# Second-layer weights loaded at other places, a third buffer for finished attention rows and for an expert's first 128 tokens, and other PSUM banks for the early-row transposes

## Chip, cores and metric

The kernel runs on one core of one Trainium2 chip. The metric is the device time of one execution in microseconds (us); lower is better.

## The reference

Block-sparse attention feeds a mixture of experts. Shapes: 4 batches, 8 heads, 768 positions, head size 64, blocks of 32 positions; 3072 tokens of 512 features; 8 experts with a hidden size of 1024.

```python
scores = q @ k.T / 8            # kept where |block_i - block_j| <= 1, where either block is
attn = softmax(scores) @ v      # the first or the last, and at 3 sampled key blocks per query block
x = attn as (3072, 512)
do = x @ w_skip > 0             # the other tokens leave as they are
e = argmax(x[do] @ w_gate); gate = softmax(x[do] @ w_gate)[e]
out[do] = x[do] + gate * (relu(x[do] @ w1[e]) @ w2[e])
```

## The kernel before

The program has two stages, and the order of the work in both is written out by hand.

**Attention.** 16 dense units (first and last query block) are followed by 44 sparse units: 22 query blocks, two units (`b` = 0 and 2) each. `sparse_step(k)` runs a software pipeline over the units: scores of unit k+2 on TensorE (`S`), row maxima on VectorE (`M`), exponentials on ScalarE (`X`), transposes (`T`, `V`) of unit k+1, the product with the values (`A`, L468) of unit k, and the normalisation (`N`, L479 to L481) and the stores (`after`, L489) of unit k-1. `N` writes a tile `xs` of finished rows, one per query block, from a pool with two buffers; `after` writes that tile to `out` with four DMAs from SyncE (SP) and transposes it on VectorE (L498) for the router. Between these, `work(q)` gives out single steps of the routing (`route`: logits, arg-max, rank, list entries) and of `look_first` (L573), which fetches the first 256 tokens of the biggest expert before attention ends and transposes them (`rows`, L596, into `xeh`, `xel`). Routing and the early transposes use one PSUM bank, `ps_r`, in turn. `fill(q)` issues loads and splits at hand-chosen steps; the last twelve weight quarters (w1 of expert 0, w2 of expert 0, w1 of expert 1) are issued there in that order, four for each matrix.

All fp32 matrices of the experts are multiplied as a high and a low part: `split_w` copies 512 columns to the high part on ScalarE (L526) and subtracts on VectorE or GpSimd (POOL) (L528). The raw weights stand in the tile that held the keys (`kts`), as a ring of three places of 2 MB: place (2p - 1) mod 3 for w1 of expert p, 2p mod 3 for w2. So a load waits until the matrix that stood there has been split or used.

**Experts.** They run one after the other, the biggest first. A `tc.Switch` jumps to code for the expert's number of tokens; each engine jumps by itself (register load of the count, branch on L1301). The first `Switch` (L1197, `arm == 0`) runs expert 0 on the early rows, with the last routing steps (`beside`) between its matmuls; `splits` cuts w2 of expert 0 from its fourth hidden slice on. Expert p then does `gemm1` (L840 to L842, one PSUM bank of five per slice `f`; `each(f)` splits slice f of its w2 beside it), the part product of its last chunk, `turn()` (transposes of the next expert's gathered rows, L630), and `gemm2` for the other chunks. `close` scales, adds the row and scatters it (L923, L73). `gather` fetches 128 rows of `out` by an indirect DMA from POOL's queue (L618); every expert has three such row tiles, in two sets that alternate. Around the end of expert p, POOL's program order is: gathers of expert p+2's second and third 128 rows, split of the next w1's last slice, load of w2 of expert p+2 (L522), end of the arm, `close_first(p)`: scatter of the first 128 rows, gather of expert p+2's first 128 rows; then the arm of expert p+1. SP loads w1 of expert p+2 in the middle of expert p.

Of the kernel before, what the change touches and what calls it, by code (L numbers as in the profile page):

```python
# [13 lines left out]
ALU = mybir.AluOpType  # L14
# [31 lines left out]
def tile_kernel(ctx, tc, qs, qd, kt, v, sb, wg, w1, w2, out):  # L46
# [368 lines left out]
    class Sparse:  # L415
# [57 lines left out]
        def N(self):  # L473
            if self.b == 0:
                Sparse.xs[self.i] = rt.tile([P, B, 2, D], F32, name="xs", bufs=2)
            xs = Sparse.xs[self.i]
            rs = ap.tile([P, 2, 2, 1], F32, name="rs")
            return [
                lambda: nc.vector.tensor_single_scalar(out=rs, in_=self.op[:, :, :, D:VD], scalar=1e-9, op=ALU.add),  # L479
                lambda: nc.vector.reciprocal(out=rs, in_=rs),  # L480
                lambda: nc.vector.tensor_tensor(out=xs[:, self.b:self.b + 2], in0=self.op[:, :, :, 0:D], in1=rs.broadcast_to([P, 2, 2, D]), op=ALU.mult),  # L481
            ]
# [90 lines left out]
    def look_first():  # L573
# [22 lines left out]
        def rows(c):  # L596
            if c == 0:
                early["t"] = [rt.tile([P, NK1, 2 * P], F32R, name=n) for n in ("xeh", "xel")]
            xh, xl = early["t"]
            tp = ps_r.tile([P, NK1, P], F32, name="rps")  # L600
            for k in range(NK1):
                nc.tensor.transpose(out=tp[:, k, :], in_=early["x"][c][:, P * k:P * k + P], identity=ident)
            cs = slice(P * c, P * c + P)
            late.append(lambda: nc.scalar.copy(out=xh[:, :, cs], in_=tp))
            after_late.append(lambda: V.tensor_tensor(out=xl[:, :, cs], in0=tp, in1=xh[:, :, cs].bitcast(F32), op=ALU.subtract))
# [92 lines left out]
    def fill(q):  # L698
# [55 lines left out]
    def sparse_step(k):  # L754
# [193 lines left out]
    def order_lists(lt=lt, lsw=lsw, size=CS):  # L948
# [24 lines left out]
    def halves(p, c, y):  # L973

        wh, wl = wview("2", p)
        cs, a = slice(P * c, P * c + P), p * CS + c
        o = os[y]
        for z in range(2):
            zs = slice(256 * z, 256 * z + 256)
            yp = yps[(y + z) % 2][:, 0:256]  # L980
            for f in range(NK2):
                for n, (l, r) in enumerate(((hh, wh), (hh, wl), (hl, wh))):
                    nc.tensor.matmul(out=yp, lhsT=l[:, f, cs], rhs=r[:, f, zs], start=(f + n == 0), stop=(f == NK2 - 1 and n == 2))
            nc.vector.scalar_tensor_tensor(out=o[:, zs], in0=yp, scalar=ltf[:, a, 1:2], in1=xs[p % 2][c][:, zs], op0=ALU.mult, op1=ALU.add)
            scatter_to(out=out.rearrange("n (z c) -> (n z) c", z=2), out_offset=bass.IndirectOffsetOnAxis(ap=ends[:, c, z:z + 1], axis=0),
                       in_=o[:, zs], in_offset=None, bounds_check=2 * N - 1, oob_is_err=False)
# [5 lines left out]
    def last_chunk(p, n, first, turn):  # L992

        def chunk(c):
            xg = xs[p % 2][c]
            with tc.If(n > CG * c + 2) as most:
# [25 lines left out]
    def full_chunks(p, n):  # L1022

        def chunk(c, last=False):
            if p == E - 1 and last:
                halves(p, c, c)
                return
            gemm2(p, c, c)
            close(p, c, c, xs[p % 2][c])
            fetch_rows(p + 2, c)  # L1030
# [15 lines left out]
    def outputs(p, n):  # L1046
# [6 lines left out]
        def turn():  # L1053
            if p + 1 < E:
                columns(xs[(p + 1) % 2], x)

# [4 lines left out]
        full_chunks(p, n)  # L1061
        if p + 2 < E:
            load_w("2", p + 2, eng=nc.gpsimd)

# [3 lines left out]
    def expert(p, n, nxt):  # L1068

        if n > CG:  # L1070
            gemm1(p, x, G * n, parts(p), few=G * (n % CG) if n % CG < 3 else 0)
# [11 lines left out]
        def turn():  # L1083
            if p + 1 < E:
                columns(xs[(p + 1) % 2], x)

# [4 lines left out]
        if p == E - 1:  # L1091
            product(p, c, G * (n - CG * c), 1)
            for y in range(c):
                if y == c - 1:
                    halves(p, y, y)
                else:
                    gemm2(p, y, y)
                    close(p, y, y, xs[p % 2][y])
            return
# [11 lines left out]
        if c == 2:  # L1111
            gemm2(p, 1, 1)
            close(p, 1, 1, xs[p % 2][1])
            fetch_rows(p + 2, 1)
        if n > 2:
            gemm2(p, 0, 0)
        if p + 2 < E:
            load_w("2", p + 2, eng=nc.gpsimd)
        announce(p + 1, nxt)

    def product(p, c, m, z):
        if m > 64:
            gemm2(p, c, z)
            close(p, c, z, xs[p % 2][c])
        else:
            gemm2_few(p, c, m, z)
            close(p, c, z, xs[p % 2][c], m)

    def gather_parts(p, m, z):

        xg, gate = xs[p % 2][0], ltf[0:m, p * CS, 1:2]
# [16 lines left out]
    def beyond():  # L1148
# [18 lines left out]
        for e in range(E):  # L1167
            a = e * LC
            n = tokens_of(e)
            with tc.If(n > CG * CS):  # L1170
# [4 lines left out]
                with tc.For_i(CS, (n + (CG - 1)) // CG, 2) as c:  # L1175
                    cur = mp.tile([P, 2, 2], I32, name="cur", bufs=1)
                    nc.vector.tensor_copy(out=cur, in_=ltx[:, bass.ds(c + a, 2), :])
                    gx = xs[0][:2]
                    for z in range(2):
# [9 lines left out]
    wt.update({"2" + t: wp2.tile([P, 4096], F32R, name=f"w2{t}") for t in "hl"})  # L1189
    xs = [[mp.tile([P, DM], F32, name=f"x{z}{c}", bufs=1) for c in range(CS)] for z in range(2)]  # L1190
    for z in range(2):
        for c in range(CS):
            nc.gpsimd.memset(xs[z][c], 0.0)
    os = [mp.tile([P, DM], F32, name=f"o{z}", bufs=1) for z in range(2)]
    yps = [ps_y.tile([P, DM], F32, name=f"yp{z}", bufs=1) for z in range(2)]
    x = [mp.tile([P, NK1, CS * P], F32R, name=n, bufs=1) for n in ("xh", "xl")]
    for arm in tc.Switch(nc.values_load(small, min_val=0, max_val=1), 2, hint="first"):  # L1197
        if arm == 0:
            px, p0, p1, d1, d1b, d2, d2b, rank, d3, d4, d5, d5b, put, d6 = last[0]()
            le, leg = early["l"]  # L1200
            load_w("2", 1, 0, 2)

# [18 lines left out]
            gemm2(0, 1, 1, range(0, 6))  # L1221
            keep_x(turn_x(xs[0][2:], ps_h, "hp"), *early["t"])
# [5 lines left out]
            columns(xs[1], x)  # L1228
            for z in range(NEAR):
                split_w("1", 1, z, 8)  # L1230
            load_w("1", 2)
            with tc.If(n0 > 2 * CG):
                gemm2(0, 0, 0)
                close(0, 2, 0, xs[0][2])
            rows(2, range(CS))
            load_w("2", 2, eng=nc.gpsimd)
        else:
            load_w("2", 1)
            for step in last[0]():
# [6 lines left out]
            clear()  # L1246
            columns(xs[0], x)
            n0 = tokens_of(0)
# [64 lines left out]
```

## Time and profile before

| | us |
|---|---|
| median of 3 runs | 526.8 (521.44 to 530.41) |
| profiled execution, whole | 517.92 |
| its span | 516.3 |
| attention, to the last row product | about 248 of it |
| TensorE busy | 448.1 (87%) |
| VectorE, ScalarE, GpSimd busy | 316.6, 247.1, 150.4 |

Times in rows are us from the span's start. PE is TensorE's matmul part, PEld its weight load, PEq or PEldq its sequencer, SP the engine that only issues DMAs. In a row the bracket tells how long the engine was idle before and what it waited for; "issue" means that it waited for nothing that the profile shows. A granted clock of 1.00 is 2.4 GHz, 0.50 is 1.2 GHz. DMA share is the mean busy share of the 16 DMA engines.

### The profile page before, as it was taken

How to read it: one execution, taken by the hardware profiler on the slowest of the kernel's cores; microseconds unless marked ns; L12 is line 12 of the kernel's file. 1: busy time of each engine (PE TensorE's matmuls, PEld its weight loads, DVE VectorE, ACT ScalarE, POOL GpSimd, SP SyncE). 2: the span in 40 equal slices, each digit the busy share in tenths (PEclk: the TensorE clock that was granted, in tenths of full speed). 3: DMA queues.
4: the chain of work that ended last, by engine and by line, in shares of the span. 5: the costliest groups of instructions: out<-in, count | busy, mean ns of one | idle time of the engine just before them, and what ended most of it. 6: DMA issues, size and time to landing. Idle time of an engine off the chain costs nothing. (4 is left out here: it accounts for less than half of the span.)

```text
span 516.3 us, 17305 instructions
## 1 busy us (share of the span) xinstructions
PE 448.1 (87%) x6594; PEld 350.5 (68%) x6594; DVE 316.6 (61%) x819; ACT 247.1 (48%) x576; POOL 150.4 (29%) x215
## 2 busy tenths in 40 slices
PE   5999998879897989997277899999999966799992
PEld 2777776656675766665167679796888853777982
DVE  2887756766776686965428257658387833494610
ACT  2444466665665666766214065455372705451500
POOL 2003333442424343433710503412314123122011
PEclk9999999999999999999678999999999987999997
DMA  8999969886989787879960605754634662811001
GB/s 283 345 274 251 222 146 225 199 217 178 222 222 228 183 221 195 216 192 284 323 224 2 241 25 182 258 207 172 233 143 150 229 228 76 329 43 48 0 18 40
DMA packets 48599, 96.48 MB, mean 187 GB/s; under 512 B 8167, under 2 KB 34920, under 8 KB 43554
## 3 DMA queue, kind: packets, MB, share of 16 engines
q1 hardware_dynamic: 43744, 73.39, 50.1%
q0 software_dynamic: 4240, 20.67, 11.6%
q8 instruction: 67, 1.10, 0.9%
q14 instruction: 114, 0.93, 0.6%
q10 hardware_dynamic: 434, 0.39, 0.2%
HBM read 85.03 MB, written 12.19 MB: 188 GB/s over the span
## 5 line engine op out<-in xcount | busy, mean ns | idle before, releaser
L455 ACT COPY pt<-tp 128x512 f32<-128x512 f32 x88 | 52.5, 599 | 57.3 <-PE tp L449 56.4
L442 ACT ACTIVATE pr<-sp,m 128x256 f32<-128x256 f32 x176 | 69.3, 483 | 2.0 <-DVE m L436 2.0
L436 DVE TENSOR_REDUCE m<-sp 128x2 f32<-128x512 f32 x88 | 56.6, 685 | 19.3 <-PE sp L429 18.3
L845 ACT ACTIVATE hh<-hp 128x256 fp32r<-128x256 f32 (+2 forms) x56 | 21.4, 381 | 89.4 <-PE hp L842 83.7
L840 PE MATMUL hp<-xh,w1h 128*128 128x256 f32 (+3 forms) x192 | 58.0, 302 | 6.1 <-DVE hl L848 2.8
L841 PE MATMUL hp<-xl,w1h 128*128 128x256 f32 (+3 forms) x192 | 57.5, 299 | 0.3 <-DVE x L1133 0.3
L429 PE MATMUL sp<-kg,q 64*32 64x256 f32 x1408 | 52.6, 386 | 5.5 <-issue 5.0
L842 PE MATMUL hp<-xh,w1l 128*128 128x256 f32 (+3 forms) x192 | 57.4, 299 | 0.0
L73 POOL DMA_INDIRECT out<-o,lt x17 | 16.8, 989 | 132.5 <-DVE o L923 89.3
L449 PEld LDWEIGHTS tp<-ident,pr 128*128 128x128 f32 x352 | 37.8, 141 | 23.0 <-issue 10.7
L449 PE MATMUL tp<-ident,pr 128*128 128x128 f32 x352 | 49.3, 281 | 4.4 <-issue 3.4
L468 PE MATMUL op<-vb,pt 128*32 128x65 f32 x1376 | 46.2, 222 | 6.1 <-issue 5.7
L468 PE MATMUL op<-va,pt 128*32 128x65 f32 x1376 | 47.0, 225 | 3.0 <-issue 2.0
L848 DVE SCALAR_TENSOR_TENSOR hl<-hp,hh 128x256 fp32r<-128x256 f32 (+2 forms) x56 | 23.4, 418 | 39.9 <-ACT hh L845 22.8
L906 PE MATMUL yp<-w2h,hh 128*128 128x512 f32 x112 | 45.0, 402 | 0.0
L908 PE MATMUL yp<-w2h,hl 128*128 128x512 f32 x112 | 44.3, 396 | 0.0
L907 PE MATMUL yp<-w2l,hh 128*128 128x512 f32 x112 | 44.3, 395 | 0.0
L212 POOL COPY kg<-kts 128x512 f32 x66 | 40.8, 628 | 6.5 <-POOL kg L212 2.3
L840 PEld LDWEIGHTS hp<-xh,w1h 128*128 128x128 f32 x192 | 36.0, 188 | 9.3 <-issue 6.2
L468 PEld LDWEIGHTS op<-va,pt 128*32 128x32 f32 x1376 | 33.4, 111 | 10.4 <-issue 9.0
L528 DVE TENSOR_TENSOR w2l<-kts,w2h 128x512 fp32r<-128x512 f32 x56 | 38.3, 688 | 3.2 <-ACT w2h L526 1.5
L468 PEld LDWEIGHTS op<-vb,pt 128*32 128x32 f32 x1376 | 34.9, 111 | 7.7 <-issue 7.7
(214 smaller groups left out, 909.4 us busy)
## 6 DMA issues: line engine op xcount, KB each, us to landing
va<-v SPq DMA_DIRECT2D x48, 260.0 KB, 4.9
vb<-v SPq DMA_DIRECT2D x48, 260.0 KB, 4.5
kts<-w SPq DMA_DIRECT2D x6, 2048.0 KB, 8.3
kts<-w POOLq DMA_DIRECT2D x6, 2048.0 KB
vt<-v SPq DMA_DIRECT2D x16, 390.0 KB, 7.5
kts<-w SPq DMA_DIRECT2D x12, 512.0 KB, 6.2
kts<-kt SPq DMA_DIRECT2D x15, 384.0 KB, 7.9
q<-qs SPq DMA_DIRECT2D x22, 256.0 KB, 3.6
```

The costliest lines, as they stand in the source:

```text
L429: nc.tensor.matmul(out=self.sp[w][32 * a:32 * a + 32, g], lhsT=qt[self.i][ws, p, :], rhs=kg[self.x][ws, p, :], start=True, stop=True)
L436: return [lambda w=w: nc.vector.tensor_reduce(out=self.mx[:, w], in_=self.sp[w], axis=AX.X, op=ALU.max, negate=True) for w in range(2)]
L442: nc.scalar.activation(out=self.pr[:, g, w], in_=self.sp[w][:, g], func=AF.Exp, bias=self.mx[:, w, g:g + 1])
L449: nc.tensor.transpose(out=tp[:, u, :], in_=self.pr[:, g, u // 2, (u % 2) * P:(u % 2) * P + P], identity=ident)
L455: nc.scalar.copy(out=self.pt[:, g], in_=self.tp[g])
L468: nc.tensor.matmul(out=self.op[32 * a:32 * a + 32, g, w, :], lhsT=self.pt[:, g, 2 * w + t, 32 * a:32 * a + 32], rhs=vt[:, 8 * (self.b + g) ...
L840: nc.tensor.matmul(out=hp[:, 0:w], lhsT=wh[:, f, k, :], rhs=xh[:, k, 0:w], start=(k == 0), stop=False)
L841: nc.tensor.matmul(out=hp[:, 0:w], lhsT=wh[:, f, k, :], rhs=xl[:, k, 0:w], start=False, stop=False)
L842: nc.tensor.matmul(out=hp[:, 0:w], lhsT=wl[:, f, k, :], rhs=xh[:, k, 0:w], start=False, stop=(k == NK1 - 1))
L906: nc.tensor.matmul(out=yp, lhsT=hh[:, f, cs], rhs=wh[:, f, :], start=(f == 0), stop=False)
L907: nc.tensor.matmul(out=yp, lhsT=hh[:, f, cs], rhs=wl[:, f, :], start=False, stop=False)
L908: nc.tensor.matmul(out=yp, lhsT=hl[:, f, cs], rhs=wh[:, f, :], start=False, stop=(f == NK2 - 1))
```

## The change

- `Sparse.N`: the tile of finished rows gets three buffers instead of two.
- `look_first`: the early transposes go to the two banks of `ps_t` (tile `tp`) instead of the one of `ps_r`.
- `sparse_step`: in the step after the last unit the routing step is run before `N` instead of after it.
- `fill` issues only w1 of expert 0. The four quarters of w2 of expert 0 are issued after the attention loop, w1 of expert 1 as one load at the start of the first arm.
- Experts: the first 128 rows have three buffers (`x0`), the other two chunks two (`x12`). `fetch_rows(p + 2, 0)` moves from `close_first(p)` to the start of expert p, and the load of w2 of expert p+2 from the end of expert p to the start of expert p+1, behind that gather.

```diff
-                Sparse.xs[self.i] = rt.tile([P, B, 2, D], F32, name="xs", bufs=2)
+                Sparse.xs[self.i] = rt.tile([P, B, 2, D], F32, name="xs", bufs=3)
...
-            tp = ps_r.tile([P, NK1, P], F32, name="rps")
+            tp = ps_t.tile([P, NK1, P], F32, name="tp")
...
-        for y in ([2 * z, 2 * z + 1] if 0 <= z < 2 else [z + 2] if 2 <= z < 10 else []):
-            which, p = (("1", 0), ("2", 0), ("1", 1))[y // 4]
-            load_w(which, p, y % 4, 4)
+        for y in ([2 * z, 2 * z + 1] if 0 <= z < 2 else []):
+            load_w("1", 0, y, 4)
...
-        mix(units[k - 1].N(), [])
+        if k < nu:
+            mix(units[k - 1].N(), [])
         pe, soon, then, pool = work(q)
         mix(soon, [])
+        if k == nu:
+            mix(units[k - 1].N(), [])
...
         run((pe, soon + then, lambda: [l() for l in pool]))
+    for y in range(4):
+        load_w("2", 0, y, 4)
     att.close()
...
+    def xr(p):
+        return [x0[p % 3]] + x12[p % 2]
+
     def rows(p, cr):
         for c in cr:
-            gather(xs[p % 2][c], lt[:, p * CS + c, 0:1])
+            gather(xr(p)[c], lt[:, p * CS + c, 0:1])
...
     def expert(p, n, nxt):
 
+        fetch_rows(p + 2, 0)
+        if p + 1 < E:
+            load_w("2", p + 1, eng=nc.gpsimd)
         if n > CG:
...
         if n > 2:
             gemm2(p, 0, 0)
-        if p + 2 < E:
-            load_w("2", p + 2, eng=nc.gpsimd)
         announce(p + 1, nxt)
...
-        close(p, 0, 0, xs[p % 2][0])
-        fetch_rows(p + 2, 0)
+        close(p, 0, 0, xr(p)[0])
...
-    xs = [[mp.tile([P, DM], F32, name=f"x{z}{c}", bufs=1) for c in range(CS)] for z in range(2)]
-    for z in range(2):
-        for c in range(CS):
-            nc.gpsimd.memset(xs[z][c], 0.0)
+    x0 = [mp.tile([P, DM], F32, name=f"x{z}0", bufs=1) for z in range(3)]
+    x12 = [[mp.tile([P, DM], F32, name=f"x{z}{c}", bufs=1) for c in range(1, CS)] for z in range(2)]
+    for t in x0 + x12[0] + x12[1]:
+        nc.gpsimd.memset(t, 0.0)
...
             le, leg = early["l"]
+            load_w("1", 1)
             load_w("2", 1, 0, 2)
...
             rows(2, range(CS))
-            load_w("2", 2, eng=nc.gpsimd)
         else:
+            load_w("1", 1)
             load_w("2", 1)
```

Elsewhere `xs[p % 2][c]` is replaced by `xr(p)[c]`.

## Rows read from the trace of the kernel before

**Rows 1.** Busy time by stage: window, its length, busy us and instruction counts of each engine, granted TensorE clock, DMA share, GB/s.
```profile
242.00:248.00 6.00, 2.59 (x126) 2.16 (x119) 0.34 (x2) 2.66 (x5) 4.59 (x4) 1.00 1.05 396
248.00:254.00 6.00, 1.49 (x11) 0.96 (x11) 4.04 (x13) 2.66 (x5) 2.25 (x3) 0.52 0.99 327
261.00:267.00 6.00, 5.81 (x31) 4.76 (x32) 0.42 (x1) 0.94 (x2) 0.00 (x0) 0.64 0.97 337
428.00:436.00 8.00, 4.52 (x18) 2.99 (x20) 3.07 (x5) 2.81 (x7) 3.07 (x3) 0.57 0.41 119
```

**Rows 2.** Timeline of VectorE at the end of attention: start, duration, line and operation, and the idle time before it.
```profile
248.27 0.42 DVE L481 TENSOR_TENSOR xs<-op,rs 128x256 f32<-128x256 f32 x1 [4.86 <-DMA out<-xs]
251.55 0.69 DVE L605 TENSOR_TENSOR xel<-rps,xeh 128x512 fp32r<-128x512 f32 x1 [1.34 <-ACT xeh L604]
252.90 0.89 DVE L307 TENSOR_TENSOR lsb<-pos,rows_of 128x384 f32<-128x384 int32 x1
```

**Rows 3.** Timeline of SP's DMA issues over the same stretch (x4 merges four issues).
```profile
235.78 3.74 SPq L522 DMA_DIRECT2D kts<-w  x4
239.62 2.57 SPq L489 DMA_DIRECT2D out<-xs  x4
242.98 4.03 SPq L522 DMA_DIRECT2D kts<-w  x4
247.67 1.87 SPq L489 DMA_DIRECT2D out<-xs  x4
250.71 3.81 SPq L522 DMA_DIRECT2D kts<-w  x4
254.61 3.39 SPq L489 DMA_DIRECT2D out<-xs  x4
```

**Rows 4.** Timeline of TensorE from the last row products to the first expert.
```profile
248.00 0.31 PE L468 MATMUL sp<-vb,pt 128*32 128x65 f32 x6 [3.41 <-issue]
249.78 1.11 PE L602 MATMUL rps<-ident,xe 128*128 128x128 f32 x4 [1.46 <-DVE xel L605]
253.94 1.48 PE L325 MATMUL rps<-phi,lsb 128*128 128x48 f32 x6 [3.04 <-DVE lsb L307]
261.19 0.57 PE L840 MATMUL hp<-xeh,w1h 128*128 128x256 f32 x1 [5.77 <-issue]
```

**Rows 5.** The branches of TensorE's sequencer, line L1301, each in a window of its own around one Switch: count, duration in ns (least, median, most), first and last start. The first is the jump into the first arm, the others those of experts 1, 5 and 6.
```profile
L1301 PEldq COMPARE_BRANCH  x1: 6195/6195/6195, 254.8 to 254.8; - x1
L1301 PEldq COMPARE_BRANCH  x2: 301/1344/2386, 306.3 to 307.8; - x2
L1301 PEldq COMPARE_BRANCH  x2: 437/3415/6393, 410.5 to 411.6; - x2
L1301 PEldq COMPARE_BRANCH  x2: 317/1434/2552, 434.8 to 435.9; - x2
```

**Rows 6.** ScalarE and POOL around the first arm: copies and subtractions for the weight splits, and the clearing of the row tiles.
```profile
270.81 0.61 ACT L526 CAST w2h<-kts 128x512 fp32r<-128x512 f32 x1
252.11 5.25 POOL L528 TENSOR_TENSOR w1l<-kts,w1h 128x512 fp32r<-128x512 f32 x4 [3.75 <-ACT w1h L526]
257.30 2.86 POOL L1193 MEMSET x<- 128x512 f32 x6
286.38 1.03 POOL L618 DMA_INDIRECT x<-out,lt  x1 [26.23 <-DVE lt L952]
```

**Rows 7.** The weight loads of line L522 as a whole: time from issue to landing.
```profile
DMA to landing us min/median/max: 5.0/6.3/8.3
```

**Rows 8.** TensorE around experts 5 and 6.
```profile
406.90 1.09 PE L630 MATMUL hp<-ident,x 128*128 128x128 f32 x8
418.41 0.47 PE L862 MATMUL hp<-w1h,xh 128*128 128x512 f32 x1 [4.38 <-issue]
431.48 1.97 PE L630 MATMUL hp<-ident,x 128*128 128x128 f32 x8 [4.40 <-DMA x<-out,lt]
434.23 4.48 PE L918 MATMUL yp<-kts,hf 128*64 128x512 f32 x16
451.24 0.41 PE L840 MATMUL hp<-xh,w1h 128*128 128x320 f32 x1 [2.75 <-DVE hl L848]
456.72 3.65 PE L918 MATMUL yp<-kts,hf 128*64 128x512 f32 x16
```

**Rows 9.** POOL's timeline from the end of expert 4 on.
```profile
413.77 1.17 POOL L618 DMA_INDIRECT x<-out,lt  x1 [0.30 <-DVE w1l L528]
418.07 0.60 POOL L522 DMA_DIRECT2D kts<-w  x1 [1.83 <-issue]
426.79 1.01 POOL L73 DMA_INDIRECT out<-o,lt  x1 [8.12 <-issue]
428.11 1.06 POOL L618 DMA_INDIRECT x<-out,lt  x1 [0.30 <-issue]
444.20 0.59 POOL L522 DMA_DIRECT2D kts<-w  x1 [3.60 <-DVE w1l L528]
```

**Rows 10.** VectorE at the start of expert 6, and SP's loads of w1 of experts 6 and 7.
```profile
450.76 0.42 DVE L848 SCALAR_TENSOR_TENSOR hl<-hp,hh 128x256 fp32r<-128x256 f32 x1 [4.52 <-issue]
407.17 0.35 SPq L522 DMA_DIRECT2D kts<-w  x1
438.92 0.35 SPq L522 DMA_DIRECT2D kts<-w  x1
```

More of the change, by code (lines that the diff above doesn't have):

```diff
@@ L983, in halves @@
                     nc.tensor.matmul(out=yp, lhsT=l[:, f, cs], rhs=r[:, f, zs], start=(f + n == 0), stop=(f == NK2 - 1 and n == 2))
-            nc.vector.scalar_tensor_tensor(out=o[:, zs], in0=yp, scalar=ltf[:, a, 1:2], in1=xs[p % 2][c][:, zs], op0=ALU.mult, op1=ALU.add)
+            nc.vector.scalar_tensor_tensor(out=o[:, zs], in0=yp, scalar=ltf[:, a, 1:2], in1=xr(p)[c][:, zs], op0=ALU.mult, op1=ALU.add)
             scatter_to(out=out.rearrange("n (z c) -> (n z) c", z=2), out_offset=bass.IndirectOffsetOnAxis(ap=ends[:, c, z:z + 1], axis=0),
@@ L994, in chunk @@
         def chunk(c):
-            xg = xs[p % 2][c]
+            xg = xr(p)[c]
             with tc.If(n > CG * c + 2) as most:
@@ L1028, in chunk @@
             gemm2(p, c, c)
-            close(p, c, c, xs[p % 2][c])
+            close(p, c, c, xr(p)[c])
             fetch_rows(p + 2, c)
@@ L1054, in turn @@
             if p + 1 < E:
-                columns(xs[(p + 1) % 2], x)
+                columns(xr(p + 1), x)
         last_chunk(p, n, lambda: split_next((0, 1)), turn)
@@ L1084, in turn @@
             if p + 1 < E:
-                columns(xs[(p + 1) % 2], x)
+                columns(xr(p + 1), x)
         c = (n - 1) // CG
@@ L1097, in expert @@
                     gemm2(p, y, y)
-                    close(p, y, y, xs[p % 2][y])
+                    close(p, y, y, xr(p)[y])
             return
@@ L1112, in expert @@
             gemm2(p, 1, 1)
-            close(p, 1, 1, xs[p % 2][1])
+            close(p, 1, 1, xr(p)[1])
             fetch_rows(p + 2, 1)
@@ L1116, in expert @@
             gemm2(p, 0, 0)
-        if p + 2 < E:
-            load_w("2", p + 2, eng=nc.gpsimd)
         announce(p + 1, nxt)
@@ L1123, in product @@
             gemm2(p, c, z)
-            close(p, c, z, xs[p % 2][c])
+            close(p, c, z, xr(p)[c])
         else:
             gemm2_few(p, c, m, z)
-            close(p, c, z, xs[p % 2][c], m)
+            close(p, c, z, xr(p)[c], m)
     def gather_parts(p, m, z):
-        xg, gate = xs[p % 2][0], ltf[0:m, p * CS, 1:2]
+        xg, gate = xr(p)[0], ltf[0:m, p * CS, 1:2]
         for j in range(1, P // m):
@@ L1177, in beyond @@
                     nc.vector.tensor_copy(out=cur, in_=ltx[:, bass.ds(c + a, 2), :])
-                    gx = xs[0][:2]
+                    gx = xr(0)[:2]
                     for z in range(2):
@@ L1221, in tile_kernel @@
             gemm2(0, 1, 1, range(0, 6))
-            keep_x(turn_x(xs[0][2:], ps_h, "hp"), *early["t"])
+            keep_x(turn_x(xr(0)[2:], ps_h, "hp"), *early["t"])
             gemm2(0, 1, 1, range(6, NK2))
@@ L1227, in tile_kernel @@
                 gemm1_tokens(0, early["t"])
-            columns(xs[1], x)
+            columns(xr(1), x)
             for z in range(NEAR):
@@ L1233, in tile_kernel @@
                 gemm2(0, 0, 0)
-                close(0, 2, 0, xs[0][2])
+                close(0, 2, 0, xr(0)[2])
             rows(2, range(CS))
-            load_w("2", 2, eng=nc.gpsimd)
         else:
+            load_w("1", 1)
             load_w("2", 1)
@@ L1246, in tile_kernel @@
             clear()
-            columns(xs[0], x)
+            columns(xr(0), x)
             n0 = tokens_of(0)
```

## The prediction

> **What bounds the kernel now.** I read the page's slices first, then busy time by stage, then the timelines of single engines where TensorE is idle, then the branches of its sequencer. TensorE is the bound nearly everywhere (87% of the span), so the change can pay only where TensorE stands still. There are two such places that it touches.
>
> The first is the end of attention. From 242 to 248 TensorE works 2.59 of 6 us, from 248 to 254 only 1.49, with the DMA engines saturated (share 1.05 and 0.99), and the clock falls to half [rows 1]. VectorE shows why: the normalisation of the last block's first unit waits 4.86 us, from 243.41 to 248.27, for the stores of the tile whose buffer it takes over [rows 2]. With two buffers that is the block before the previous one, whose four stores SP issued only at 239.62, behind four weight quarters [rows 3]. Behind the waiting instruction on VectorE stands the subtraction that frees the single `ps_r` bank, so the second early transposition waits 1.46 us more, to 249.78 [rows 4]. From there a chain runs through ScalarE, the subtraction (to 252.24), the last normalisation, the routing's one-hot rows (L307, to 253.79), the `put` matmuls at 253.94 and the jump into the first arm, which takes TensorE's sequencer 6.2 us, to the first expert matmul at 261.19 [rows 2, 4, 5].
>
> The second is experts 5 and 6. Before expert 6's rows are transposed TensorE waits 4.40 us for a gather [rows 8], which POOL issued at 428.11, behind a scatter that came 8.12 us after the load of w2 of expert 6 [rows 9]. In 428 to 436 the clock is 0.57 of full [rows 1]. Inside expert 6 a further 2.75 us go, while VectorE is between two arms and idle 4.52 us [rows 8, 10].
>
> **The change, part by part. End of attention.** A third buffer makes the last block wait for the block three back, stored long before: 4.86 us of waiting go, and VectorE's next work starts at 243.4. The early transposes in `ps_t` no longer need the subtraction. What is late next is TensorE's own stream: it stands 3.41 us in the middle of a run of equal matmuls, without a semaphore, from 244.59 to 248.00 [rows 4]. I take this, like the 6.2 us jump, for a wait for instructions while the DMA engines are full, since jumps take 2.4 and 2.55 us in quiet stretches but 6.4 where a 2 MB weight load had been issued at 407.17, 4.4 us earlier [rows 5, 10]. Without w2 of expert 0, issued at 242.98 before [rows 3], the DMA engines have only the rest of w1 and small stores in 244 to 252. So I take 1.0 us for the stall (bounds 0 and 3.41) and 2.6 us for the jump (bounds 2.4 and 6.2).
>
> The new chain: the stall would start at 244.6; it and the last six matmuls end the row products at 245.8; the second transposition follows. From its start to the `put` it took 4.16 us (249.78 to 253.94); the three normalisation operations now follow L307 instead of preceding it, which saves 0.75, and at full clock the transposition is some 0.3 shorter: 3.1 us, so `put` at 248.9. The jump begins 0.86 us later as before (253.94 to 254.8): 249.8, plus 2.6, plus the 0.2 before the first matmul (254.8 + 6.2 to 261.19): 252.6. The gain is 261.19 - 252.6 = **8.6 us**. Bounds: both waits as before give 244.6 + 3.4 + 0.2 + 3.1 + 0.86 + 6.2 + 0.2 = 258.6, a gain of 2.6; none and 2.4 give 251.4, a gain of 9.8. The half clock lasts into 261 to 267 (0.64 [rows 1]); if shorter idle times spare it, up to 2 us more, counted only in the upper end.
>
> The Trainium skill speaks against the first of these terms (Runtime: NRT & Kernel Launch, "Instruction fetch mechanics"): an engine streams straight code by itself and crossing a block is mostly hidden; only a taken branch outside its window must wait for a fetch. By that rule the 3.41 us stall is something else and stays, and the sum would be 2.4 us smaller; for the jump rule and row agree.
>
> What hides the moved loads: w2 of expert 0. SP finishes the last block's four stores near 252 (normalised by 249.5; 2.6 us for four issues [rows 3]), then issues the four quarters from 252 to 256, and a load lands 6.3 us (5.0 to 8.3) later [rows 7]: 258 to 262. ScalarE first splits it at 270.81, 9.6 us after the first expert matmul [rows 6], now near 262. The cover is 4 us for the first quarter, and the later ones are used later. Gone, each us late is a us lost, because the one-hot rows of the last routing queue on VectorE behind the splits. w1 of expert 1 moves behind it and is split some 40 us later: nothing. That it is one issue instead of four saves SP some 3 us, off the path. The seventh clearing on POOL costs 2.86/6 = 0.5 us, hidden in POOL's idle 26 us [rows 6]; POOL's own subtractions start earlier, since ScalarE is not held.
>
> **Experts.** The gather of expert 6's first rows moves to the start of expert 4, and those of its other rows were issued by 413.77 [rows 9]; so the 4.40 us wait goes. The transposes and the 16 part-product matmuls follow at full clock: 1.97 - 1.09 and 4.48 - 3.65 us [rows 8], together 1.7 us. The jump of expert 6, issued 1.7 us after that product starts and 2.55 long [rows 5], ends about 0.4 us after the product and takes a little back: gain **5.7 us** (bounds 0, if something else holds ScalarE or the weights there, and 6.1). In the other experts the gather was early enough; no gain.
>
> The load of w2 moves on POOL past the arm's end, the scatter, the next jump and a gather. Its own wait for the w1 split in its place (3.60 us at 444.20 [rows 9]) no longer stands ahead of the scatter. It lands some 10 us into an expert that lasts 20 or more, and is split in the next: nothing. Behind it wait the next gathers, needed an expert later: nothing. It no longer runs beside VectorE's jump into expert 6, which had w1 of expert 7 (438.92) and this load (444.20) before it [rows 9, 10]. Of the 2.75 us I take half, **1.3** (bounds 0 and 2.75); the w1 load stays. The 4.38 us before expert 5 [rows 8] stay: its w1 load is not moved.
>
> The Trainium skill has a rule against shorter jumps altogether (DMA: Bandwidth & Descriptors, "Queues, rings and completion order"): a DMA engine takes turns between queues packet by packet, and instruction refill has a queue of its own, so a weight load should hardly hold it up. By that rule both fetch terms vanish, which is the first rival; the 6.2 and 6.4 us beside 2.4 speak against it, with two cases only.
>
> **Sum.** 8.6 + 5.7 + 1.3 = 15.6 us of 517.92 (the profiled execution): 502.3. That execution lies 8.9 under the median of the runs, 526.8; what the runs have more I can't place, so the difference is subtracted from the median: **511 us**, 3.0% less.
>
> **Rivals.**
> - Waits for instructions stay as long as they are (stall 3.4, jump 6.2, VectorE's jump 4.5): 2.6 + 5.7 = 8.3 us gained, **518.5**. For it: only two slow jumps, and SP still sends 5 MB around the first arm. Chance 0.24.
> - The expert part gives nothing, because another wait takes the gather's place (the w1 slices, or ScalarE's copies before them): 8.6 gained, **518**. Against it: w1 of expert 6 was issued at 407.17 [rows 10]. Chance 0.10.
> - Slower: w2 of expert 0 comes too late. Place: ScalarE's first split, then VectorE's one-hot rows, then TensorE in the first arm, a us for each us. It eats the 14.3 us of the two main gains when the first quarter lands at 276 instead of 258, 24 us after its issue at 252; at 282 it costs 20 us and the kernel takes 511 + 20 = **531**. The longest landing on record is 8.3 us [rows 7]. Chance 0.04.
> - More than forecast: no stall at all, full clock at the first expert, all of the 2.75: 9.8 + 2 + 6.1 + 2.75 = 20.6, **506**. Chance 0.10.
>
> **Numbers.** The forecast has 0.52. A measurement here tells about 2% from no change, that is 516.3. Faster by more: forecast and the last case, 0.62; within 2%: the first two rivals and a little, 0.34; slower: 0.04. The range runs from the gain of 20.6 with some us for the spread of the runs to the rivals at 518 with the same: 502 to 522.
>
> **What would show it.** Right: no wait of L481 on stores; the second early transposition directly behind the last row products; first expert matmul near 252; a jump into the first arm near 2.6 us; the w2 split of expert 0 not waiting on a DMA; no gather ahead of expert 6's transposes and clock 1.00 there. Wrong: the jump or the stall as long as before, ScalarE waiting for `kts<-w` in the first arm, or TensorE idle elsewhere in experts 5 and 6 for the same time.

## The result and the profile after

The kernel after takes 506.85 us in the median (504.96 to 514.35, four runs), the kernel before on the same chip 525.21: ratio 0.967, interval 0.960 to 0.974. In a second set of runs it took 506.07 against 519.56: 0.971 (0.961 to 0.981). The profiled execution of after took 504.96 us with a span of 503.3, 13.0 less than the profiled one of before. The direction, the size and both places were as forecast (511.0); what the steps gave differs in several terms.

The stages again (window, length, busy us and instructions of each engine, granted clock, DMA share, GB/s), answering to [rows 1]:
```profile
242.00:248.00 6.00, 3.21 (x122) 2.45 (x111) 3.92 (x10) 3.06 (x6) 3.74 (x4) 0.95 0.88 320
248.00:254.00 6.00, 1.49 (x6) 1.36 (x6) 3.70 (x9) 2.26 (x5) 6.00 (x5) 0.50 0.23 55
254.00:260.00 6.00, 5.45 (x32) 4.51 (x32) 0.42 (x1) 0.97 (x2) 3.75 (x8) 0.70 0.70 208
428.00:432.00 4.00, 4.00 (x18) 4.00 (x19) 1.63 (x1) 0.00 (x0) 1.08 (x1) 0.57 0.94 377
```
VectorE, SP and TensorE at the end of attention (timelines: start, duration, line, operation, idle before and what ended it), answering to [rows 2 to 4]:
```profile
243.17 0.42 DVE L481 TENSOR_TENSOR xs<-op,rs 128x256 f32<-128x256 f32 x1
...
245.81 1.02 DVE L315 TENSOR_TENSOR col<-cols,cols_of 128x72 f32<-128x72 int32 x1
246.87 1.27 DVE L311 TENSOR_TENSOR phi<-col,pays 128x144 f32<-128x144 f32 x1
248.22 0.69 DVE L605 TENSOR_TENSOR xel<-tp,xeh 128x512 fp32r<-128x512 f32 x1
248.83 0.86 DVE L307 TENSOR_TENSOR lsb<-pos,rows_of 128x384 f32<-128x384 int32 x1
```
```profile
240.42 12.91 SPq L489 DMA_DIRECT2D out<-xs  x12
254.11 10.04 SPq L522 DMA_DIRECT2D kts<-w  x5
```
```profile
246.65 0.32 PE L468 MATMUL sp<-vb,pt 128*32 128x65 f32 x6 [2.35 <-issue]
246.90 0.66 PE L602 MATMUL tp<-ident,xe 128*128 128x128 f32 x4
249.84 1.49 PE L325 MATMUL rps<-phi,lsb 128*128 128x48 f32 x6 [2.27 <-DVE rs L479]
254.55 0.55 PE L844 MATMUL hp<-xeh,w1h 128*128 128x256 f32 x1 [3.23 <-issue]
```
L481 no longer waits for stores, and the second early transposition starts directly behind the last row products. Yet TensorE still stands 2.35 us among those products, though SP issues only stores from 240.42 to 253.3 and the next weights from 254.11 on. The DMA engines are still full in that stall (share 1.00 from 244.30 to 246.65, before 1.06 in its stall): the last quarter of w1 of expert 0, issued at 239.99, landed at 247.31. The DMA share falls to 0.23 in 248 to 254, but the clock still falls to half there. ScalarE's first split of w2 and POOL:
```profile
263.72 0.61 ACT L526 CAST w2h<-kts 128x512 fp32r<-128x512 f32 x1
244.26 10.23 POOL L528 TENSOR_TENSOR w1l<-kts,w1h 128x512 fp32r<-128x512 f32 x8 [8.42 <-ACT w1h L526]
254.43 3.32 POOL L1198 MEMSET x<- 128x512 f32 x7
```
The split does not wait for the later load (its first quarter landed at 258.38). The branches of TensorE's sequencer, now L1307 (first arm, experts 1, 5, 6), answering to [rows 5]:
```profile
L1307 PEldq COMPARE_BRANCH  x1: 3535/3535/3535, 250.7 to 250.7; - x1
L1307 PEldq COMPARE_BRANCH  x1: 2286/2286/2286, 301.1 to 301.1; - x1
L1307 PEldq COMPARE_BRANCH  x2: 446/2629/4812, 404.8 to 406.0; - x2
L1307 PEldq COMPARE_BRANCH  x1: 4762/4762/4762, 422.8 to 422.8; - x1
```
The jump into the first arm fell from 6.2 to 3.54 us; the one into expert 6 rose from 2.55 to 4.76. TensorE and POOL around experts 5 and 6, answering to [rows 8, 9]:
```profile
411.15 0.66 PE L866 MATMUL hp<-w1h,xh 128*128 128x512 f32 x1 [2.61 <-issue]
419.67 1.04 PE L630 MATMUL hp<-ident,x 128*128 128x128 f32 x8
421.07 3.65 PE L922 MATMUL yp<-kts,hf 128*64 128x512 f32 x16
427.88 0.38 PE L844 MATMUL hp<-xh,w1h 128*128 128x320 f32 x1 [3.16 <-DVE w1l L528]
```
```profile
412.85 1.02 POOL L73 DMA_INDIRECT out<-o,lt  x1 [2.10 <-DVE o L927]
415.64 1.03 POOL L618 DMA_INDIRECT x<-out,lt  x1 [1.77 <-issue]
416.78 0.58 POOL L522 DMA_DIRECT2D kts<-w  x1
...
438.13 0.59 POOL L522 DMA_DIRECT2D kts<-w  x1 [2.32 <-issue]
```
The transposes (419.67) no longer wait for the gather and run at full clock, as does the part product; then 3.16 us are idle in the longer jump, and the clock is 0.57 after it.

**By stretches.** One execution differs from the next, so each stretch of TensorE's timeline is given below over all profiled executions that have the same code in it (us, from the first instruction named to the next): before's code in the kernel before and the experiments that kept that part, after's likewise.

| Stretch | before's code | after's code |
|---|---|---|
| first early transposition to first expert matmul | 18.3 (one) | 11.8 to 14.6, middle 12.8 (eight) |
| expert 0 | 49.2 to 50.0 (four) | 49.2 to 51.6 (eight, without added traffic) |
| experts 1 to 4 | 107.9 to 110.1 (five) | 107.1 to 109.3 (four, without added traffic) |
| expert 5, to the first product of expert 6 | 19.3 to 22.2 (five) | 15.1 to 16.8 (six) |
| expert 6, to the first product of expert 7 | 34.7 to 36.6 (five) | 32.5 to 33.0 (six) |
| expert 7, to TensorE's last matmul | 32.5 to 32.6 | 32.5 to 32.6 |

So some 5.5 us come from the end of attention (against a single execution of before's code), some 4 to 5 from expert 5, some 3 from expert 6, and the rest shows no difference that stands out of its spread. In the two profiled executions alone it is 6.3, 3.7 and 2.0.

### The profile page after: what moved, and what is told of

Its sections match the earlier page's. It is cut to its first block, busy times and chain, and to the rows that moved or that the text cites. A ratio compares the mean times of both kernels' runs of the same rounds, so it can differ in the third digit from the quotient of the medians.

```text
span 503.3 us, 17274 instructions
## 1 busy us (share of the span) xinstructions
PE 447.4 (89%) x6594; PEld 352.3 (70%) x6594; DVE 317.6 (63%) x819; ACT 246.3 (49%) x576; POOL 152.4 (30%) x216
## 3 DMA queue, kind: packets, MB, share of 16 engines
q8 instruction: 66, 1.08, 0.9%
## 5 line engine op out<-in xcount | busy, mean ns | idle before, releaser
L436 DVE TENSOR_REDUCE m<-sp 128x2 f32<-128x512 f32 x88 | 56.6, 684 | 19.3 <-PE sp L429 18.3
L449 PEld LDWEIGHTS tp<-ident,pr 128*128 128x128 f32 x352 | 38.7, 143 | 23.8 <-issue 13.5
L449 PE MATMUL tp<-ident,pr 128*128 128x128 f32 x352 | 50.5, 285 | 5.0 <-issue 4.2
L73 POOL DMA_INDIRECT out<-o,lt x17 | 16.8, 988 | 125.0 <-DVE o L927 108.5
L468 PE MATMUL op<-vb,pt 128*32 128x65 f32 x1376 | 47.3, 224 | 5.6 <-issue 4.7
L852 DVE SCALAR_TENSOR_TENSOR hl<-hp,hh 128x256 fp32r<-128x256 f32 (+2 forms) x56 | 23.4, 418 | 34.7 <-ACT hh L849 19.1
```

What stands on the lines that cost most here:

```text
L436: return [lambda w=w: nc.vector.tensor_reduce(out=self.mx[:, w], in_=self.sp[w], axis=AX.X, op=ALU.max, negate=True) for w in range(2)]
L449: nc.tensor.transpose(out=tp[:, u, :], in_=self.pr[:, g, u // 2, (u % 2) * P:(u % 2) * P + P], identity=ident)
L468: nc.tensor.matmul(out=self.op[32 * a:32 * a + 32, g, w, :], lhsT=self.pt[:, g, 2 * w + t, 32 * a:32 * a + 32], rhs=vt[:, 8 * (self.b + g) ...
```

## Experiments: the end of attention

**The third buffer alone.** Before, with one line changed:
```
-                Sparse.xs[self.i] = rt.tile([P, B, 2, D], F32, name="xs", bufs=2)
+                Sparse.xs[self.i] = rt.tile([P, B, 2, D], F32, name="xs", bufs=3)
```


> The kernel before with a third buffer for the finished rows alone. Theory (TensorE's stall in the last row products and its jump into the first arm are long because of the weight loads beside them): the 4.86 us wait of L481 goes, but the stall stays near 3.4 us and the jump near 6.2 us, since w2 of expert 0 is still loaded there; first expert matmul near 259.3 instead of 261.19, the whole kernel 2 us faster (0.996 of before). Rival (the buffer alone does it, loads do not matter): first expert matmul near 255, kernel 6 to 7 us faster (0.987).

Measured: 518.88 us, ratio 0.992 (0.987 to 0.996); the stretch from the first early transposition to the first expert matmul 16.2 us, the stall in the row products 3.00, the jump into the first arm 5.96. L481 no longer waits. Stall and jump stayed long, as the theory said; in the stretch the buffer is worth some 2 us by itself.

**The loads alone.** Before, with w2 of expert 0 and w1 of expert 1 issued later:
```
+        for y in ([2 * z, 2 * z + 1] if 0 <= z < 2 else []):
+            load_w("1", 0, y, 4)
...
+    for y in range(4):
+        load_w("2", 0, y, 4)
...
+            load_w("1", 1)
```


> The kernel before with only the loads of w2 of expert 0 and w1 of expert 1 moved behind the attention loop. Theory: L481 still waits for the stores of the tile, but these land sooner without the load behind them (by about 246), the stall is near 2.4 us and the jump near 3.5 us as in the changed kernel; first expert matmul near 256.5, 4 to 5 us faster (0.991). Rival (loads do not matter): first expert matmul stays at 261, same time.

Measured: 519.33 us, ratio 0.992 (0.987 to 0.996); stretch 15.7. The jump fell to 3.46 us, L481 still waited 4.44, and the stall stayed 3.41. So with these loads gone the jump was short, while the stall was not.

**Buffer and banks, loads as before.** The third buffer, and in addition:
```
-            tp = ps_r.tile([P, NK1, P], F32, name="rps")
+            tp = ps_t.tile([P, NK1, P], F32, name="tp")
```
and the last `N()` behind `soon`.

> The kernel before with third buffer, other banks for the early transposes and the routing step ahead of the last normalisation, weight loads as before. Theory: stall 3.4, jump 6.2; first expert matmul near 258.6, 2.6 us faster (0.995). Rival (loads do not matter): near 254.6, 6.6 us faster (0.987).

Measured: 520.9 us, ratio 0.995 (0.990 to 1.000); stretch 13.9: stall 2.88, jump 4.21. The time is the theory's (0.995); the stretch lies between theory and rival: the stall hardly moved, and the jump is 1.75 us shorter than with the buffer alone. The instruction packet of that jump, of which more below, begins 1.80 us after the jump's start here and 3.49 with the buffer alone; why it comes earlier with the loads in the same place, these runs don't show.

**Both together.** The edits of the last two runs; experts as before.

> The whole attention part of the change (buffer, banks, order, later loads), experts as before. Theory: first expert matmul near 254.6 as in the changed kernel, the 4.40 us wait for the gather before expert 6 and the 2.75 us in it stay; 6.6 us faster (0.987), the other half of the gain belongs to the experts. Rival (the experts' part gives nothing of its own, its waits would have gone anyway with another alignment of loads): as fast as the changed kernel (0.967 to 0.975).

Measured: 519.32 us, ratio 0.989 (0.978 to 1.000); stretch 13.0, jump 3.82; the wait for the gather (2.85 us) and the stall of 3.30 us inside expert 6, where TensorE waits for VectorE, stay in the experts. What the front gives is there; the rest of the change's gain is the experts'. In time these four runs can't be told from each other (0.989 to 0.995, with overlapping intervals), and each stretch is one execution.

**After, with these loads back in attention.** The reverse of the second diff.

> The changed kernel with only the loads of w2 of expert 0 and w1 of expert 1 back in the last attention steps. Theory (a jump or a stretch of code is slowed by loads in flight): the jump into the first arm is 4 to 6 us instead of 3.5, the stretch from the first early transposition to the first expert matmul 14 us instead of 12.0, the experts as in the changed kernel; about 2 us slower than that, 0.971 of before. Rival (the loads do not matter once buffer and banks are there): 12.0 us, as fast as the changed kernel.

Measured: 507.99 us, ratio 0.976 (0.970 to 0.981); stretch 12.8, stall 2.17, jump 4.71. That stretch lies within after's 11.8 to 14.6, and the interval overlaps those of after: beside the other two edits the moved loads shorten the jump (4.71 to between 3.4 and 4.0), but what they are worth in the time can't be told from nothing.

**After, with only one quarter of w1 of expert 0 loaded** (the products read what the tile held for the rest):
```
+            if y == 0:
+                load_w("1", 0, y, 4)
```


> The changed kernel without three of the four quarters of w1 of expert 0, which leaves expert 0's result wrong and takes 1.5 MB of traffic out of the end of attention. Theory (stall and jump last as long as the transfers beside them): the stall in the last row products below 1 us instead of 2.35, the jump into the first arm 2.4 to 3.0 us instead of 3.5; 10 to 11 us from the first early transposition to the first expert matmul instead of 12.0. Rival (they are what they are): 2.3 and 3.5 us, 12.0.

Measured: one run of 508.71 us. TensorE's stall and the `put`:
```profile
248.38 0.32 PE L468 MATMUL sp<-vb,pt 128*32 128x65 f32 x6 [0.72 <-issue]
...
253.22 1.49 PE L325 MATMUL rps<-phi,lsb 128*128 128x48 f32 x6 [3.93 <-DVE rs L479]
```
0.72 us is the shortest stall seen, but one execution; with after's own loads it was 1.15 to 3.19 in eight. The jump was 3.31, not 2.4 to 3.0; the stores of finished rows are still beside it, but no run took them away. And the `put` now waits 3.93 us for VectorE (below, on what was not expected).

## Experiments: experts 5 and 6

**w2 loads back at the end of an expert, early gather kept.**
```
+        if p + 2 < E:
+            load_w("2", p + 2, eng=nc.gpsimd)
...
-        if p + 1 < E:
-            load_w("2", p + 1, eng=nc.gpsimd)
```


> The changed kernel with only the load of w2 of expert p+2 back at the end of expert p. Theory (the early gather removes the wait before expert 6's transposes, the moved load shortens VectorE's jump and lengthens TensorE's): no wait for the gather, TensorE's jump into expert 6 at 2.3 to 2.9 us instead of 4.76, so that expert starts 2 us sooner, but the stall of 2.5 to 3.8 us inside it is back; as fast as the changed kernel within 1.5 us. Rival (the moved load is what removes the wait): 4 us or more slower than the changed kernel.

Measured: 508.52 us, ratio 0.974 (0.966 to 0.982); expert 5 15.8 us, expert 6 34.8. TensorE, and POOL with its two loads:
```profile
420.49 1.37 PE L630 MATMUL hp<-ident,x 128*128 128x128 f32 x8
...
438.73 0.41 PE L844 MATMUL hp<-xh,w1h 128*128 128x320 f32 x1 [3.08 <-DVE hl L852]
```
```profile
411.88 0.60 POOL L522 DMA_DIRECT2D kts<-w  x1 [1.83 <-issue]
419.89 1.01 POOL L73 DMA_INDIRECT out<-o,lt  x1 [7.41 <-issue]
...
431.43 0.59 POOL L522 DMA_DIRECT2D kts<-w  x1 [1.19 <-DVE w1l L528]
```
The scatter is late again, yet the transposes do not wait: the early gather suffices. The jump into expert 6, 12 us behind the load's issue, took 2.32 us. The stall inside expert 6 is back, with a load of w2 of expert 7 issued at 431.43, 7 us before it ends; before had it at 444.20, 6.6 us before [rows 9, 10]; after issues it at 438.13, behind the place, and has no stall there. Over all 14 executions it is the same: the stall is there in the seven with this load 6.3 to 7.8 us before VectorE goes on, and in none of the seven others. The time can't be told from after's.

**The gather late again, w2 loads as after.**
```
-        fetch_rows(p + 2, 0)
...
+        fetch_rows(p + 2, 0)
```


> The changed kernel with only the gather of an expert's first 128 rows back behind close_first. Theory (the early gather is what removes the wait): the wait before expert 6's transposes is back at 3 us or more, 4 to 5 us slower than the changed kernel (0.976 of before). Rival (the moved w2 load is enough, since POOL's scatter and gather no longer come behind a load in flight: they would be issued near 414 and land by 418, before the transposes at 419.7): no wait, as fast as the changed kernel.

Measured: 505.28 us, ratio 0.970 (0.964 to 0.977); expert 5 15.9 us, expert 6 30.8. POOL, TensorE, its jump into expert 6, and the window behind it:
```profile
412.51 1.01 POOL L73 DMA_INDIRECT out<-o,lt  x1 [2.10 <-DVE o L927]
413.83 1.03 POOL L618 DMA_INDIRECT x<-out,lt  x1 [0.30 <-issue]
```
```profile
419.60 1.04 PE L630 MATMUL hp<-ident,x 128*128 128x128 f32 x8
...
426.98 0.39 PE L844 MATMUL hp<-xh,w1h 128*128 128x320 f32 x1 [2.32 <-DVE w1l L528]
```
```profile
L1307 PEldq COMPARE_BRANCH  x1: 3922/3922/3922, 422.6 to 422.6; - x1
```
```profile
428.00:432.00 4.00, 4.00 (x29) 4.00 (x28) 1.56 (x1) 0.00 (x0) 1.02 (x1) 1.00 0.92 373
```
The rival is right: without a weight load ahead of it on POOL the scatter comes at 412.51, the gather right behind it, and nothing waits. By what path the load held POOL's scatter these runs don't show: the gathers that POOL issues right behind the same load in after (from 417.66) did not wait. Each of the two edits removes the gather wait by itself; the third tile for an expert's first rows is not needed beside the moved load. Most of the 2.2 us less in expert 6 lies in the clock, 1.00 here where after had 0.57 in the same window; that is one execution, with a jump of 3.92 us although the load is in flight as in after.

**w2 loads issued by SP at the end of an expert.** The diff of the run with w2 at the end, without `eng=nc.gpsimd`.

> The kernel after, with one change: the second weights of the next expert but one are issued by SyncE at the end of an expert, not by GpSimd at the start of the next. Theory (the jump into an expert costs PE 2.1 to 2.9 us while the DMA engines are idle and 4 us or more while they move a weight load; after paid 4.76 at 422.8 because the 2 MB issued at 416.8 were in flight): issued at about 412, they have landed by then, the jump into expert 6 takes 2.3 to 3.2 us, expert 5 takes 15.8 us to the first product of expert 6 instead of 16.8, GpSimd's scatter at the end of expert 5 no longer stands behind a weight load (it waited 7.4 us when GpSimd issued the load at 411.9, which gave 3.1 us of stall inside expert 6), and expert 6 keeps its 33.0 us or less. Time 503 to 506 us, 1 to 2 us below after. Rival (the jump's length has nothing to do with the transfer in flight): jump into expert 6 stays at 4.5 to 5 us, time as after, 505 to 507.

Measured: four runs from 508.6 to 526.2 us, too far apart to set against the forecast of 503 to 506, and the profiled one (517.55) reached its first expert matmul 11 us later than after, at 265.52. So it is compared by stretches alone: expert 5 12.7 us, expert 6 36.0, experts 1 to 4 110.4. The branches into experts 3 and 6 (the longest in each row), and TensorE inside expert 6:
```profile
L1310 PEldq COMPARE_BRANCH  x2: 301/2710/5120, 367.0 to 368.1; - x2
L1310 PEldq COMPARE_BRANCH  x2: 399/1318/2237, 434.0 to 435.2; - x2
```
```profile
450.43 0.53 PE L844 MATMUL hp<-xh,w1h 128*128 128x320 f32 x1 [3.55 <-DVE hl L852]
```
The jump into expert 6 went to 2.24 us as expected, but the one into expert 3 rose to 5.12 (after: 3.40), and the stall in expert 6 is back. From the first expert matmul to the end of the span it takes 250.2 us, after 248.8 and, in its other execution, 249.1: nothing gained. No version here beats after beyond its interval; the one with the late gather can't be told from it, with an edit less.

**After once more**, beside the last one.

> The kernel after once more, unchanged, for a comparison on the same chip with the version whose second weights SyncE issues. Both theories: 504.5 to 507.5 us; jump into expert 6 4.5 to 5 us, no wait of the first product of expert 5 for its rows, start of the early rows' work anywhere between 238 and 248 us.

Measured: 506.07 us, as said; jump into expert 6 4.72 us, no wait for the gather. Its stall was 2.98 us and the jump into the first arm 4.0, against 2.35 and 3.54 in the first execution of the same code.

## Experiments: what a jump's length follows

**Traffic in rows of 6 KB at a quiet jump.** After, with the turned tokens of expert 1 copied to a scratch in DRAM behind `columns(xr(1), x)`:
```
+            for t in x:
+                nc.sync.dma_start(out=dram.tile([P, NK1, CS * P], F32, name="spare", bufs=2), in_=t.bitcast(F32))
```


> The kernel after, with 1.5 MB of traffic that computes nothing (the turned tokens of expert 1, copied from SBUF to a scratch in DRAM) put in flight at the one jump where the DMA engines are idle: PE's jump into expert 1, 2.29 us at 301.1 with a DMA share of 0.01. Theory (a jump's length follows the load on the DMA engines): with a share of 0.8 or more in its first 2.4 us the jump takes 4 to 6 us; the stretch from expert 0's first product to expert 1's, 49.2 us, grows to 50.5 to 52.5, since about 1 us of the jump lay beside a wait for the first weights' low parts. Rival (the jump's length belongs to the place, the arm's size or the clock, and only looked related to the load): 2.1 to 2.6 us, stretch 49.2 to 49.9 as in all the other runs without a slow arm.

Measured: 509.93 us, ratio 0.982 (0.971 to 0.993); stretch 49.4 us, as the rival said. The jump into expert 1, and the packets from 299 to 301.25 (count, MB, how many are short):
```profile
L1309 PEldq COMPARE_BRANCH  x1: 2451/2451/2451, 301.1 to 301.1; - x1
```
```profile
DMA packets 163, 0.92 MB, mean 407 GB/s; under 512 B 16, under 2 KB 16, under 8 KB 161
```
Full engines (share 1.06 also in the first 2.4 us of the jump) and a jump of 2.45 us: the theory "a jump's length follows the DMA share" fell here. The DMA view shows what it does go with. A packet is one piece that a DMA engine moves. The view has queues named "instruction"; on q8 go packets of 16 KB (66 of them, 1.08 MB, in after). That these are TensorE's instructions is inferred from their timing, as the view names no engine. A packet is counted in the window in which it begins: 23.4% of 16 engines over 0.25 us, in the first row below, are 0.94 us, longer than the window. The last q8 packet before the end of this jump began between 301.00 and 301.25, as the jump begins; in after's long jump into expert 6 (begun at 422.8) it began between 425.00 and 425.25; in before's short one (435.9) between 435.75 and 436.00. The rows of these three windows:
```profile
q8 instruction: 1, 0.02, 23.4%
```
```profile
q8 instruction: 1, 0.02, 24.1%
```
```profile
q8 instruction: 1, 0.02, 32.3%
```
Over the 105 branches above 1.8 us of the runs so far (the packet's beginning after the branch's start, and the branch's length, in us):

| packet began | jumps | length, least / median / most |
|---|---|---|
| up to 0.2 | 43 | 1.9 / 2.4 / 3.7 |
| 0.2 to 1 | 31 | 2.7 / 3.3 / 4.0 |
| 1 to 2 | 9 | 3.4 / 3.7 / 4.2 |
| over 2 | 22 | 4.7 / 5.1 / 6.5 |

Where the packet begins over 1 us late, the jump ends 2.3 us or more behind that, in the median 2.4. Counted from the packet's end, it holds for all 105: the packet takes 0.9 to 2.1 us, and the jump ends 1.2 to 2.1 us after it has, in the median 1.4, be it 1.9 us long or 6.5. So both count, how late the packet begins and how long it takes: in before's jump into expert 5 (6.39 us) it began 2.5 us after the start and took 2.0. The stall in the last row products obeys the same rule: the packet began in 245.50 to 245.75 in before and TensorE went on at 248.00; in after 244.25 to 244.50 and 246.65; with a quarter of w1, 246.00 to 246.25 and 248.38. In all 14 executions TensorE went on 2.3 to 2.6 us after that packet began, 1.2 to 1.6 after its end.

**Traffic in rows of 16 KB at the same jump.** Expert 0's second weights are copied in place of the tokens:
```
+            nc.sync.dma_start(out=dram.tile([P, P], F32, name="spare", bufs=1), in_=x[0][:, 0, 0:P].bitcast(F32))
+            nc.sync.dma_start(out=dram.tile([P, 4096], F32, name="spare2", bufs=1), in_=wt["2h"].bitcast(F32))
```


> The kernel after, with 2 MB of traffic that computes nothing at PE's jump into expert 1, as in the run with the copied tokens, but in rows of 16 KB (expert 0's second weights, copied from SBUF to a scratch in DRAM) in place of rows of 6 KB. There the engines were full (share 1.08) and the jump still took 2.45 us, because the 16 KB packet on the instruction queue landed 0.1 us after the jump's start; over the other runs a jump ends about 2.3 us after that packet lands. Theory (what delays the packet is the length of the other packets on the same DMA engine): it lands 0.5 to 2.0 us after the start, and the jump takes 2.8 to 4.3 us. Rival (copies out of SBUF don't hold up the packet whatever their length; only loads from DRAM, or GpSimd's queue, do): it lands at most 0.2 us after the start, and the jump takes 2.2 to 2.5 us. Both: the jump's length less the packet's landing stays 2.0 to 2.6 us.

Measured: 504.32 us, ratio 0.970 (0.950 to 0.989). The branch, the packets from 297 to 302, and the instruction packet, in 302.40 to 302.65:
```profile
L1309 PEldq COMPARE_BRANCH  x1: 5411/5411/5411, 299.4 to 299.4; - x1
```
```profile
DMA packets 119, 1.68 MB, mean 336 GB/s; under 512 B 16, under 2 KB 16, under 8 KB 16
```
```profile
q8 instruction: 1, 0.02, 23.4%
```
What the expectation calls the packet's landing is its beginning, as above. It began 3.1 us after the start, took 0.94, and the jump took 5.41, more than the theory's 4.3; the stretch from expert 0's first product to expert 1's took 51.8 us (the table's 49.2 to 51.6 reach nearly as far, so the branch is the evidence). So traffic alone lengthens the quietest jump, and full engines with 6 KB packets did not. That it is the length of the copies' rows is not shown: both copies also held up SP's load of w1 of expert 2, 2 MB from DRAM in rows of 16 KB. In after it was issued at 278.03 and had landed at 286.70, long before the jump; with the copied tokens it was issued at 300.13, 1 us before the jump, and here at 295.50, 3.9 us before it. That load alone may be the reason, the rival's "loads from DRAM", and no run has the copies without it.

## Why the prediction was right, and where not

- **L481's wait and the bank.** Right: both waits went. The transposition to the `put` took 2.94 us (forecast 3.1).
- **Stall in the row products, 1.0 assumed.** Wrong: 2.35 in the profiled execution, 1.15 to 3.19 in eight with after's code, and 3.41 with the loads moved and nothing else. The step that failed is "without w2 of expert 0 the DMA engines have only the rest of w1 and small stores": the rest of w1, which landed until 247.31, and the stores kept them full through the stall (share 1.00). At 2.35 the upper bound, 3.41, was nearer than the 1.0 or the lower bound. The rule of the Trainium skill that I weighed against this term (Runtime: NRT & Kernel Launch, "Instruction fetch mechanics"), that crossing a block in straight code is mostly hidden, had the sum right on this point, as the stall mostly stayed. Its "mostly hidden" does not fit this place: in all 14 executions TensorE stood 0.72 to 3.41 us here and went on 1.2 to 1.6 us after an instruction packet's end.
- **Jump into the first arm, 2.6 assumed.** Right in direction (6.2 to 3.54; the loads alone 3.46), 0.9 us short; the last block's stores, issued from 250.46 on, are in flight beside it, which is the likely reason, and the run without three quarters of w1 shows 3.31 with them. The forecast gave all of the shorter jump to the moved loads. With buffer and banks in place they shorten it by about 1 us (4.71 with the loads back), and that gain can't be seen in the time. With the stall 2 us of the 8.6 are missing; 6.6 were measured from 261.19 to 254.55, inside the bounds of 2.6 to 9.8.
- **Cover of the later w2 load.** Right: issued 254.11 to 258.25, no wait in the first arm.
- **Expert 5, 5.7 us.** Half right. Wait, transposes (1.04) and part product (3.65) came out as worked out. What failed is the step on the jump ("ends about 0.4 us after the product"; by its own rows 0.6, 1.69 + 2.55 - 3.65): I costed the moved load of w2 at nothing, and it is in flight when TensorE jumps into expert 6, 4.76 us in place of 2.55. In six executions with after's code that jump took 4.7 to 5.5, and 3.92 with the gather late; with the load elsewhere 2.2 to 2.9. Net 3.7 us in the profiled pair. And I credited the gather alone; the moved load does the same by itself. The wait before expert 5, said to stay at 4.38, was 2.61: before's code has 2.6 to 4.5 in five executions, after's 2.6 to 3.3 in six, so no gain is shown.
- **VectorE's stall in expert 6, 1.3.** Mis-sized: all of the 2.75 went (32.5 to 33.0 us in place of 34.7 to 36.6), as w2 of expert 7 is issued behind it. The half clock behind the longer jump took part of that back; with the late gather, where it stayed full, expert 6 took 30.8.
- **The sum and the median.** 15.6 forecast, 13.0 in the profiled pair, 18.4 and 13.5 between the medians of the two sets. In the profiled pair the front and expert 5 gave 2.0 us each less than forecast, expert 6 gave 0.7 more, so errors partly cancel. The profiled execution of before was a short one: from the first expert matmul to the end 255.1 us, against 257.1 to 259.6 in the four experiments that leave experts 1 to 7 as they were. Subtracting from the median was right, but part of the agreement with it is luck.
- **The rivals.** "Waits for instructions stay": half true, the stall did. The rule of the Trainium skill that queues take turns packet by packet (DMA: Bandwidth & Descriptors, "Queues, rings and completion order") would fit the runs in kind, as the refill began 0.1 us after the jump's start beside packets of 6 KB and 3.1 us beside 16 KB, though length was not isolated. My reading of it, that a load would hardly hold up a refill, does not fit: in after's jump into expert 6 it began 2.3 us after the start. The slower rival's place never waited.

## What to carry to other kernels

A load that is moved off one wait is in flight at some later moment: look which jumps and gathers fall between its issue and its landing (4.3 to 12.4 us over the loads of L522 in after), and cost it there. Before crediting an edit with a removed wait, ask whether another edit of the same change removes it too; a chain of load, scatter and gather on one queue can be broken at either end. And read a stall of an engine "without a semaphore" beside the instruction queues in the DMA view: when their packet begins, and how long it takes, tells when the engine goes on.

## What was not expected of the hardware

A jump of TensorE cost 2.0 to 2.9 us in the 30 cases with hardly anything else moving (DMA share of the other queues under 0.05), and up to 6.5 otherwise; in every case it ended 1.2 to 2.1 us after a 16 KB packet on the instruction queue had ended. Straight code pays too: 0.72 to 3.41 us at one place in 14 executions.

Two of VectorE's small operations before the `put`, L315 and L311, took 1.02 and 1.27 us in after (rows above) while POOL subtracted without a pause (eight in 10.23 us, 1.28 each); in before, with POOL idle, on the same shapes:
```profile
249.64 0.22 DVE L315 TENSOR_TENSOR col<-cols,cols_of 128x72 f32<-128x72 int32 x1
249.90 0.31 DVE L311 TENSOR_TENSOR phi<-col,pays 128x144 f32<-128x144 f32 x1
```
That is 1.8 us more, which the forecast did not have. In after it cost nothing: L311 ended at 248.14, and ScalarE's copy (L604), which the next operation L605 needs, at 248.18. It shows once the stall is short: with a quarter of w1 the copy was ready at 250.09, and L605 began 1.4 us later, behind L311 (1.26 us there):
```profile
247.60 0.58 ACT L604 CAST xeh<-tp 128x512 fp32r<-128x512 f32 x1 [1.39 <-PE tp L602]
```
```profile
249.51 0.58 ACT L604 CAST xeh<-tp 128x512 fp32r<-128x512 f32 x1
251.46 0.68 DVE L605 TENSOR_TENSOR xel<-tp,xeh 128x512 fp32r<-128x512 f32 x1
```
The first row is after's, the other two are from the run with a quarter of w1. The Trainium skill (SBUF — State Buffer, "Who interferes with whom") says that a VectorE operation with two SBUF inputs and a GpSimd operation that reads SBUF share a port pair, and the second waits until the first has finished; the durations agree, but no run here took POOL's subtractions away.
